# Fused attention and two expert layers: the opening pair taken head by head, maxima ordered by head, conversions spread over steps

## The chip, the cores and the metric

The kernel runs on one core of one Trainium2 chip. A core has TensorE (PE, the matrix engine, with PEld for its weight loads), VectorE (DVE), ScalarE (ACT), GpSimd (POOL) and SyncE (SP, which here only issues transfers). They run their own instruction queues in order and wait for each other by semaphores. The metric is the device time of one execution in microseconds; lower is better.

## The reference

```
q_pool = q.reshape(B, H, S // 2, 2, D).mean(axis=3)      # B 4, H 8, S 1152, D 64
scores = matmul(q_pool, k^T) / sqrt(D);  scores -= max(scores, axis=-1)
attn   = exp(scores);  attn /= sum(attn, axis=-1) + 1e-9
x      = matmul(attn, v), heads side by side               # 2304 tokens x 512
x      = (h - tanh(h)) @ w_out,      h = x @ w_in          # d_ff 2048
out    = (h * sigmoid(1.702 h)) @ w_out2, h = x @ w_in2
```

All products are carried in two parts: an operand is split into a rounded high part and the rest (names ending in h and l), and three products stand for one. The expert weights come as 64-bit numbers and are put together from their two 32-bit words by four bit operations on VectorE before they are split.

## The kernel before

**Pairs and steps.** The 32 heads are worked in 16 pairs, two heads side by side on the 128 partitions, head 0 of a pair on partitions 0 to 63 and head 1 on 64 to 127. A pair takes 18 steps, nine tiles of 128 keys for each head. In step g, `scores(g)` makes the transposed scores of one key tile for all 576 pooled queries (four products of 288 columns, lines 348 and 349) and ScalarE takes the exponential from the score banks twice, once whole (`pf`) and once rounded (`ph`). `rest(g-1)` subtracts the two (`pl`, line 372) on VectorE, or on GpSimd in steps 5 and 14. `pv(g-3)` multiplies with v: six products, or for each third tile two products in full precision that take the place of four (lines 394 and 384). The last one of a head is copied out by ScalarE (line 400, `u`).

**The row of maxima.** The negated maximum of each query is a 65th row of the second score operand (`q3`), so it has to be known before the scores. `max_tile(p, j, x)` multiplies one 128-column piece of the block-diagonal `bdqs` (both heads' queries) with half of the keys and VectorE reduces the result to one column of `mt` (lines 304, 308). 18 half tiles make a pair. Their PSUM pool holds one tile. `max_rows` takes the minimum of the two halves, transposes and sends the row by four transfers (line 324). For pairs from 2 on the half tiles stand one in a step, from step 13 of two pairs ahead to step 12 of the pair ahead; for pair 1 in the first 13 steps of pair 0; for pair 0 ahead of all, as nine whole tiles of three 384-column products.

**What sets the order.** Each engine's order is that in which the Python code calls; `plan` and `when` are tables of (pairs from the end or ahead, step) at which preparation of later pairs and the first eight expert weight blocks are called. `stack` sends a head's high and low parts into the score operands by six transfers on SyncE. The low part of k (`prep_kl`, line 284, on GpSimd) has one buffer, so it waits for the stack ahead of it. `normalise` (line 444) multiplies the finished pair by the reciprocals of its sums. Weight blocks are loaded by SyncE (line 123) into two buffers and converted by ScalarE (Abs, line 136), VectorE (lines 137, 141, 148, 152), ScalarE (line 159) and GpSimd (line 160), grouped as load, first two, last two, split.

Of the kernel before, what the change touches and what calls it, by code (L numbers as in the profile page):

```python
# [7 lines left out]
F32 = mybir.dt.float32  # L8
# [20 lines left out]
def tile_pooled_attention_two_moe(  # L29
# [72 lines left out]
    bdqs = [part(6 * S + i * S, QJ, 128) for i in range(2)]  # L102
# [26 lines left out]
    def convert_steps(raw, hi, lo, shape):  # L129
        box = {}  # L130

        def s0():
# [7 lines left out]
            )  # L140
            nc.vector.scalar_tensor_tensor(  # L141
                out=box["t"], in0=top, scalar=-0x40000000, in1=box["t"],
# [3 lines left out]
        def s1():  # L146
# [4 lines left out]
            )  # L151
            nc.vector.scalar_tensor_tensor(  # L152
# [13 lines left out]
        return [s0, s1, split] if raw.dtype == I32 else [s32]  # L166
# [6 lines left out]
    def piece(kind, n):  # L173
# [24 lines left out]
        return [ld, cv(0), cv(1), cv(2)]  # L198

    def attention(ctx: ExitStack):  # L200
# [18 lines left out]
        nc.vector.memset(f32(bdqs[0][:]), 0.0)  # L219
# [16 lines left out]
        def load_q(p):  # L236
            qraw[p] = ap.tile([128, 2, SP], F32, tag="qr", name="qr")
            nc.sync.dma_start(out=qraw[p], in_=q[p // NPB, p % NPB])

        def load_k(p):  # L240
            kraw[p] = ap.tile([128, S], F32, tag="kr", name="kr", bufs=2)
            nc.sync.dma_start(out=kraw[p], in_=k[p // NPB, p % NPB])
# [5 lines left out]
        def prep_qs(p, eng=None):  # L248
# [8 lines left out]
            (eng or nc.vector).tensor_add(pairs[p]["qs"], qraw[p][:, 0], qraw[p][:, 1])  # L257
# [8 lines left out]
        def prep_bdq(p, s):  # L266
            r = slice(64 * s, 64 * s + 64)
            nc.scalar.activation(
                bdqs[p % 2][r, :, r],
                pairs[p]["qs"][r, :].rearrange("p (j c) -> p j c", j=QJ), AF.Copy)  # L270
# [4 lines left out]

        def first_bdq():
            for s in range(2):
                r = slice(64 * s, 64 * s + 64)
                x = [qraw[0][r, e].rearrange("p (j c) -> p j c", j=QJ) for e in range(2)]
                nc.vector.tensor_add(bdqs[0][r, :, r], *x)  # L280
# [18 lines left out]
        def max_tile(p, j, x=0, pool=None, parts=2, n=HB):  # L299
            d = pairs[p]  # L300
            mx = (pool or ps_mx).tile([128, parts, 512], F32, tag="mx", name="mx")
            for a in range(parts):
                k0 = (x * parts + a) * n
                nc.tensor.matmul(  # L304
                    mx[:, a, 0:n], bdqs[p % 2][:, j, :], d["kh"][:, k0:k0 + n],
# [5 lines left out]
        def max_rows(p, queues=(nc.sync, nc.sync)):  # L311
            d = pairs[p]
            tt = ap.tile([128, 32], F32R, tag="tt", name="tt", bufs=2)
            if p > 0:
                mt = d["mt"]
                nc.vector.tensor_tensor(
                    mt[:, 0:QJ], f32(mt[:, 0:QJ]), f32(mt[:, 16:16 + QJ]), op=ALU.min)
# [484 lines left out]
```

## Time and profile before

| | us |
|---|---|
| time before, median of 3 runs (lowest, highest) | 1352.25 (1352.02, 1352.96) |
| the profiled execution: its time; its span | 1352.21; 1350.4 |
| PE busy in the span (share) | 1299.2 (96%) |
| DVE busy | 993.7 (74%) |
| ACT busy | 749.0 (55%) |
| POOL busy | 353.7 (26%) |

The span runs from the first to the last instruction of the profiled execution; its time is 1.8 us longer. Matmuls are pipelined and an instruction's end is modelled, so the distance from one start to the next says more on PE than a duration. In rows of a timeline the first number is the start, the second the time from the start of a group to its end, then engine, line, operation, output and inputs, count, and in brackets how long the engine had stood idle and what it waited for. PEclk is the granted clock as a share of full speed.

### The profile page before, as it was taken

How to read it: one execution, taken by the hardware profiler on the slowest of the kernel's cores; microseconds unless marked ns; L12 is line 12 of the kernel's file. 1: busy time of each engine (PE TensorE's matmuls, PEld its weight loads, DVE VectorE, ACT ScalarE, POOL GpSimd, SP SyncE). 2: the span in 40 equal slices, each digit the busy share in tenths (PEclk: the TensorE clock that was granted, in tenths of full speed). 3: DMA queues.
4: the chain of work that ended last, by engine and by line, in shares of the span. 5: the costliest groups of instructions: out<-in, count | busy, mean ns of one | idle time of the engine just before them, and what ended most of it. 6: DMA issues, size and time to landing. Idle time of an engine off the chain costs nothing.

```text
span 1350.4 us, 18699 instructions
## 1 busy us (share of the span) xinstructions
PE 1299.2 (96%) x6999; PEld 1154.7 (86%) x6999; DVE 993.7 (74%) x1242; ACT 749.0 (55%) x1143; POOL 353.7 (26%) x275
## 2 busy tenths in 40 slices
PE   5899999999999998989999999999999999999998
PEld 3899999999989987879889889888788888888887
DVE  6677777778887876899999999999843555645433
ACT  2577777777777766767665655666533322222211
POOL 6123333232333334224333333323110110110000
PEclk9999999999999998999999999999999999999999
DMA  7466666666666562111111111111111111111002
GB/s 186 121 166 169 163 165 170 167 164 155 162 150 173 128 144 63 57 48 32 47 48 32 48 47 32 47 48 32 48 47 32 47 47 32 60 35 32 24 32 86
DMA packets 59129, 117.56 MB, mean 87 GB/s; under 512 B 24992, under 2 KB 29088, under 8 KB 59040
## 3 DMA queue, kind: packets, MB, share of 16 engines
q1 hardware_dynamic: 59004, 116.38, 32.5%
q8 instruction: 55, 0.90, 0.3%
q14 instruction: 34, 0.28, 0.1%
q10 hardware_dynamic: 36, 0.00, 0.0%
HBM read 66.58 MB, written 4.79 MB: 53 GB/s over the span
## 4 chain that ended last, share of the span: by engine, by line
PE 55%; DVE 26%; ACT 7%; issue 4%; SPq 3%; DMA 3%; POOL 1%; DVEq 0%; ACTq 0%; POOLq 0%
PE y L697 16%; PE h L604 14%; PE pv L394 8%; PE mx L304 5%; PE pv L384 5%; PE sc L349 4%; PE sc L348 4%; DVE gg L661 3%; DVE mt L308 3%; DVE xb L710 2%; DVE wt L141 2%; DVE gg L645 2%; DVE wt L137 2%; DVE wt L148 2%; DVE wt L152 2%
## 5 line engine op out<-in xcount | busy, mean ns | idle before, releaser
L308 DVE TENSOR_REDUCE mt<-mx 128x1 fp32r<-128x576 f32 (+1 forms) x279 | 215.9, 775 | 99.7 <-PE mx L304 95.8
L354 ACT ACTIVATE pf<-sc 128x576 f32<-128x576 f32 x288 | 188.5, 654 | 150.0 <-PE sc L349 132.9
L604 PE MATMUL h<-hl,big 128*128 128x512 f32 (+1 forms) x940 | 211.6, 377 | 0.0
L604 PEld LDWEIGHTS h<-hl,big 128*128 128x128 f32 x940 | 174.0, 188 | 28.6
L348 PE MATMUL sc<-q,big 128*128 128x288 f32 x576 | 185.4, 335 | 1.5 <-DVE mt L308 1.5
L697 PE MATMUL y<-g,big 128*128 128x512 f32 (+1 forms) x780 | 177.4, 370 | 6.3 <-POOL g L616 5.4
L697 PE MATMUL y<-big,g 128*128 128x512 f32 x702 | 174.1, 392 | 3.2 <-DVE xb L710 3.2
L349 PE MATMUL sc<-q,a 65*128 65x288 f32 x576 | 165.6, 301 | 2.0 <-DMA q<-tt 2.0
L697 PEld LDWEIGHTS y<-g,big 128*128 128x128 f32 x780 | 141.8, 188 | 28.9 <-POOL g L616 8.1
L616 POOL TENSOR_TENSOR g<-gg,g 128x1024 fp32r<-128x1024 f32 (+1 forms) x40 | 87.7, 2191 | 275.5 <-ACT g L614 267.8
L697 PEld LDWEIGHTS y<-big,g 128*128 128x128 f32 x702 | 132.7, 189 | 31.1 <-DVE xb L710 3.6
L304 PE MATMUL mx<-kh,big 128*128 128x288 f32 (+1 forms) x567 | 134.5, 322 | 23.8 <-DVE mt L308 16.8
L372 DVE TENSOR_TENSOR pl<-pf,ph 128x576 fp32r<-128x576 f32 x160 | 146.2, 915 | 3.3 <-PE sc L349 1.8
L394 PE MATMUL pv<-ph,big 128*128 128x288 f32 x768 | 142.9, 297 | 5.6 <-ACT u L400 5.6
L614 ACT ACTIVATE g<-gg 128x1024 fp32r<-128x1024 f32 (+1 forms) x80 | 78.0, 974 | 115.8 <-PE y L697 105.7
L604 PE MATMUL h<-hl,w 128*128 128x512 f32 (+1 forms) x564 | 127.0, 377 | 0.0
L304 PEld LDWEIGHTS mx<-kh,big 128*128 128x128 f32 x567 | 95.0, 199 | 36.6 <-DVE mt L308 28.7
L160 POOL TENSOR_TENSOR big<-wt,big 128x512 fp32r<-128x512 f32 x46 | 67.7, 1480 | 219.8 <-ACT big L159 219.8
L710 DVE TENSOR_TENSOR xb<-xb,y 128x512 f32<-128x512 f32 (+1 forms) x114 | 71.1, 654 | 70.0 <-PE y L697 70.0
L394 PEld LDWEIGHTS pv<-ph,big 128*128 128x128 f32 x768 | 117.0, 190 | 6.0 <-ACT u L400 5.8
L364 ACT ACTIVATE ph<-sc 128x576 fp32r<-128x576 f32 x186 | 121.3, 652 | 0.0
L604 PEld LDWEIGHTS h<-hl,w 128*128 128x128 f32 x564 | 104.4, 188 | 17.1
(80 smaller groups left out, 2105.9 us busy)
## 6 DMA issues: line engine op xcount, KB each, us to landing
raw<-in_moe_w_in_dram SPq DMA_DIRECT2D x32, 512.0 KB
raw<-in_moe_w_out_dram SPq DMA_DIRECT2D x32, 512.0 KB
qr<-in_q_dram SPq DMA_DIRECT2D x16, 576.0 KB
kr<-in_k_dram SPq DMA_DIRECT2D x16, 576.0 KB
big<-kh SPq DMA_DIRECT2D x32, 288.0 KB
q<-qh SPq DMA_DIRECT2D x64, 144.0 KB
big<-kl SPq DMA_DIRECT2D x32, 288.0 KB
a<-kh SPq DMA_DIRECT2D x32, 288.0 KB
```

What stands on the lines that cost most here:

```text
L304: nc.tensor.matmul(mx[:, a, 0:n], bdqs[p % 2][:, j, :], d["kh"][:, k0:k0 + n], start=True, stop=True)
L308: nc.vector.tensor_reduce(d["mt"][:, c:c + 1], mx[:, :, 0:n], AX.XY, ALU.max, negate=True)
L348: nc.tensor.matmul(sc[:, x, 0:HB], a1[:, ks], q2[:, xs], start=True, stop=False)
L349: nc.tensor.matmul(sc[:, x, 0:HB], a2[:, ks], q3[:, xs], start=False, stop=True)
L354: nc.scalar.activation(both(pf), sc[:, :, 0:HB], AF.Exp, scale=SCALE)
L364: nc.scalar.activation(both(ph), sc[:, :, 0:HB], AF.Exp, scale=SCALE)
L372: eng.tensor_tensor(pl, pf, f32(ph[:]), op=ALU.subtract)
L394: nc.tensor.matmul(accs[hd][x], w[:, t, :], r[:, x * HB:(x + 1) * HB], start=(t == 0 and n == 0), stop=(t == KT - 1 and n == 2))
L604: nc.tensor.matmul(hb[:, j, 0:TBS[b]], wi[:, c, w, :], x[r][c], start=(k == 0), stop=(k == 3 * NKC - 1))
L616: eng.tensor_tensor(gt[:, :, 1, :], g, f32(gt[:, :, 0, :]), op=ALU.subtract)
L697: nc.tensor.matmul(ys[m][:, 0:w], lhsT, rhs, start=(fp == 0 and k == 0), stop=(fp == 1 and k == 5))
L710: nc.vector.tensor_add(dst, dst, ys[m][:, 0:w])
```

## The change

- `bdqs` is laid out by head: columns 0 to 575 are head 0's queries, 576 to 1151 head 1's, and a 128-column piece is cut across (piece 4 holds both heads). Head 0's row is then complete after five of nine pieces, and `max_rows(p, s)` is called for one head at a time: head 0 at step 13 of the pair ahead, head 1 at step 3 of the pair itself, four transfers each.
- The half tiles of a pair stand in 18 steps that begin at step 4 of the pair ahead, nine steps later than before.
- Pair 0 is opened by head: q and k are loaded in halves of 64 partitions, head 0's maxima are taken from `qh` and `kh` themselves (`first_max`, five tiles), then one tile of head 1; head 1's other eight half tiles stand in steps 0 to 2, with two PSUM buffers.
- `keep_warm(n)` issues n products of 512 columns on the zeroed `bdqs[1]` into a bank that nobody reads: 11 ahead of the first tile, one behind each tile of head 0, 14 behind head 1's first.
- Pair 0 and 1 have a table of their own (`opening`). In the others `stack(n, 1)` moves from step 13 to step 10, `normalise` is halved onto steps 2 and 5, some of the rest moves by a step.
- The four bit operations of a weight block are four calls and each has its own step; all loads and steps of the first eight blocks are placed anew. In the expert layers they are grouped as before (`joined`).
- GpSimd takes five subtractions in pair 0, two in the middle pairs, none in pair 15, and there four roundings instead of six.

```diff
-    bdqs = [part(6 * S + i * S, QJ, 128) for i in range(2)]
+    bdqs = [part(6 * S + i * S, S) for i in range(2)]
...
-        return [s0, s1, split] if raw.dtype == I32 else [s32]
+        return [shift, sign, flush, tail, split] if raw.dtype == I32 else [s32]
...
+        def first_max(s, j, x, pool, parts, n):
+            d = pairs[0]
+            r = slice(64 * s, 64 * s + 64)
+            m = min(128, SP - 128 * j)
+            mx = pool.tile([128, parts, 512], F32, tag="mx", name="mx")
+            for a in range(parts):
+                k0 = (x * parts + a) * n
+                nc.tensor.matmul(
+                    mx[0:m, a, 0:n], d["qh"][r, 128 * j:128 * j + m], d["kh"][r, k0:k0 + n],
+                    start=True, stop=True)
+            c = 16 * x + 5 * s + j
+            nc.vector.tensor_reduce(
+                d["mt"][0:m, c:c + 1], mx[0:m, :, 0:n], AX.XY, ALU.max, negate=True)
...
-        POOL_SUB = (5, 14)
-        pool_cast = range(NPAIR * NS - NS + 2, NPAIR * NS, 3)
+        pool_sub = {0: (5, 8, 11, 14, 17), NPAIR - 1: ()}
+        pool_cast = [(NPAIR - 1) * NS + i for i in (3, 6, 9, 12)]
...
-            ("o", 1, (-2, 14), (-1, 1), (-1, 3), (-1, 5)),
+            ("o", 1, (-2, 4), (-1, 5), (-1, 6), (-1, 7), (-1, 8), (-1, 9)),
...
+        q_sum(nc.vector, "qh", low)
+        k_high(nc.scalar, low, 0)
+        k_high(nc.gpsimd, low, 1)
+        q_sum(nc.vector, "qs", low)
+        nc.vector.tensor_sub(d0["ql"][low], d0["qs"][low], f32(d0["qh"][low]))
+        k_low(low, 0)
+        k_low(low, 1)
+        stack(0, 0)
...
+            def keep_warm(n):
+                for _ in range(n):
+                    nc.tensor.matmul(
+                        warm, bdqs[1][:, 0:128], bdqs[1][:, 0:512], start=True, stop=True)
+
+            keep_warm(11)
+            for j in range(5):
+                first_max(0, j, 0, ps_first, 3, 384)
+                keep_warm(1)
+            new_pair(1)
+            prep_kh(1, 0)
+            prep_kh(1, 1)
+            max_rows(0, 0, (nc.sync, nc.scalar, nc.sync, nc.scalar))
+            first_max(1, 0, 0, ps_first, 3, 384)
+            keep_warm(14)
+        load_v(0, 0)
+        prep_v(0, 0)
+        load_q(1)
+        stack(0, 1)
...
-                at = (n - 1) * NS - 5 + h if n > 1 else 13 * h // 18
-                max_at[at] = max_at.get(at, ()) + ((n, *divmod(h, 2)),)
+                max_at.setdefault(NS * n - 14 + h, []).append(
+                    lambda n=n, h=h: max_tile(n, *divmod(h, 2)))
...
+            (1, 2): [(stack, 0)], (1, 3): [(prep_v, 0)], (1, 10): [(stack, 1)],
+            (1, 12): [(prep_v, 1)], (1, 13): [(max_rows, 0)], (0, 3): [(max_rows, 1)],
...
-            if p > 1 and i == 4:
-                normalise(p - 2)
+            if p > 1 and i in (2, 5):
+                normalise(p - 2, [i // 3])
```

PE's queue from its first product to step 3 of pair 0, before (mx is a maximum tile, sc a score tile, pv the value banks):

```order
L304 MATMUL mx<-kh,big 128x384 x27
L348 MATMUL sc<-q_0_79,big 128x288
L349 MATMUL sc<-q_0_80,a_0_78 128x288
L348 MATMUL sc<-q_0_79,big 128x288
L349 MATMUL sc<-q_0_80,a_0_78 128x288
L304 MATMUL mx<-kh,big 128x288 x4
```

And now; warm is the bank of the zero products:

```order
L568 MATMUL warm<-big 128x512 x11
L338 MATMUL mx<-kh,qh 128x384 x3
L568 MATMUL warm<-big 128x512
...
L338 MATMUL mx<-kh,qh 64x384 x3
L568 MATMUL warm<-big 128x512
L338 MATMUL mx<-kh,qh 128x384 x3
L568 MATMUL warm<-big 128x512 x14
L392 MATMUL sc<-q_0_79,big 128x288
L393 MATMUL sc<-q_0_80,a_0_78 128x288
L392 MATMUL sc<-q_0_79,big 128x288
L393 MATMUL sc<-q_0_80,a_0_78 128x288
L338 MATMUL mx<-kh,qh 128x288 x6
```

Nine tiles ahead of the first score have become six with zero products between them, and three half tiles a step follow the first scores.

VectorE's queue in steps 2 to 7 of a middle pair with a weight block under conversion, before (xb is the normalised output, wt the weight under conversion):

```order
L308 TENSOR_REDUCE mt_90<-mx 128x1 x2
L372 TENSOR_TENSOR pl<-pf,ph 128x576
L308 TENSOR_REDUCE mt_90<-mx 128x1
L372 TENSOR_TENSOR pl<-pf,ph 128x576
L444 TENSOR_TENSOR xb_64<-u,rbd 128x320
L444 TENSOR_TENSOR xb_65<-u,rbd 128x256
L308 TENSOR_REDUCE mt_90<-mx 128x1 x2
L137 TENSOR_SCALAR wt<-raw 128x512
L141 SCALAR_TENSOR_TENSOR wt<-raw,wt 128x512
L308 TENSOR_REDUCE mt_90<-mx 128x1
```

And now, in steps 2 to 6:

```order
L328 TENSOR_REDUCE mt_90<-mx 128x1
L493 TENSOR_TENSOR xb_64<-u,rbd 128x320
L328 TENSOR_REDUCE mt_90<-mx 128x1
L416 TENSOR_TENSOR pl<-pf,ph 128x576
L351 TENSOR_TENSOR mt_90<-mt_90 128x5
L356 STREAM_TRANSPOSE tt<-mt_90 128x32
L328 TENSOR_REDUCE mt_92<-mx 128x1
L416 TENSOR_TENSOR pl<-pf,ph 128x576
L328 TENSOR_REDUCE mt_92<-mx 128x1
L493 TENSOR_TENSOR xb_65<-u,rbd 128x256
L328 TENSOR_REDUCE mt_92<-mx 128x1
L137 TENSOR_SCALAR wt<-raw 128x512
```

The two halves of the normalisation have moved apart, onto steps without a subtraction, the minimum and transpose of head 1 have come in at step 3, and one bit operation stands where there were two.

SyncE's queue from the row transfers (tt) of pair 15 on, before (raw is a weight block):

```order
L324 DMA q_0_80<-tt 1x9x32 x2
L324 DMA q_1_83<-tt 1x9x32 x2
L292 DMA big<-kh 64x1152
L293 DMA q_1_82<-qh 64x576
L294 DMA big<-kl 64x1152
L295 DMA q_1_82<-qh 64x576
L296 DMA a_1_81<-kh 64x1152
L297 DMA q_1_83<-ql 64x576
L123 DMA raw<-in_moe_w_out_dram 128x1024 x2
```

And now, from the first of these two weight loads (step 4 of pair 14) on, to head 1's row in step 3 of pair 15:

```order
L123 DMA raw<-in_moe_w_out_dram 128x1024
...
L312 DMA big<-kh 64x1152
L313 DMA q_1_82<-qh 64x576
L314 DMA big<-kl 64x1152
...
L478 DMA rbd<-rd 64x576 x2
L367 DMA q_0_80<-tt 1x5x32 x2
L367 DMA q_0_80<-tt 1x4x32 x2
L123 DMA raw<-in_moe_w_out_dram 128x1024
L367 DMA q_1_83<-tt 1x4x32 x2
L367 DMA q_1_83<-tt 1x5x32 x2
```

One of the two loads now stands ahead of the last stack and the last rows, the other between the two rows.

## Rows read from the trace of the kernel before

**Rows 1.** Windows: length, busy time of PE, PEld, DVE, ACT, POOL, PEclk, DMA.

```profile
58.00:504.00 446.00, 438.61 (x2941) 412.69 (x2940) 357.88 (x515) 320.71 (x567) 145.48 (x134) 1.00 0.63 157
...
537.00:1350.40 813.40, 796.38 (x3748) 687.02 (x3746) 579.84 (x659) 388.76 (x509) 170.40 (x97) 1.00 0.14 43
```

**Rows 2.** The page, 40 slices of the span: granted clock in tenths.

```profile
PEclk9999999999999998999999999999999999999999
```

**Rows 3.** The chain that ended last: start, length, what.

```profile
39.66 0.24 PE sc L349
...
45.38 0.14 PE sc L349
...
80.86 0.97 PE pv L384 x4
...
85.84 0.97 PE pv L384 x4
```

**Rows 4.** Timeline of PE in pair 0.

```profile
24.41 0.58 PE L349 MATMUL sc<-q,a 65*128 65x288 f32 x1 [1.99 <-DMA q<-tt]
...
57.77 0.29 PE L348 MATMUL sc<-q,big 128*128 128x288 f32 x1
```

**Rows 5.** Timelines of DVE and then SyncE, opening.

```profile
1.05 1.02 DVE L219 MEMSET big<- 128x1152 f32 x1 [1.05 <-PEq L787]
...
4.82 1.52 DVE L280 TENSOR_TENSOR big<-qr 64x576 fp32r<-64x576 f32 x2 [2.67 <-DMA qr<-in_q_dram]
...
17.62 2.62 DVE L308 TENSOR_REDUCE mt<-mx 128x1 fp32r<-128x1152 f32 x2 [0.16 <-PE mx L304]
...
21.79 0.21 DVE L318 STREAM_TRANSPOSE tt<-mt 128x32 f32<-128x32 f32 x1
...
33.95 0.76 DVE L257 TENSOR_TENSOR qs<-qr 128x576 f32<-128x576 f32 x1 [2.80 <-DMA qr<-in_q_dram]
...
28.73 1.25 SPq L238 DMA_DIRECT2D qr<-in_q_dram  x1
```

**Rows 6.** Timelines of PE, DVE and POOL in middle pairs.

```profile
109.31 0.53 PE L304 MATMUL mx<-kh,big 128*128 128x288 f32 x2 [0.20 <-DVE mt L308]
...
139.99 0.53 PE L304 MATMUL mx<-kh,big 128*128 128x288 f32 x2 [0.22 <-DVE mt L308]
...
341.35 0.52 PE L304 MATMUL mx<-kh,big 128*128 128x288 f32 x2 [1.04 <-DVE mt L308]
...
130.43 0.75 DVE L372 TENSOR_TENSOR pl<-pf,ph 128x576 fp32r<-128x576 f32 x1
...
135.67 1.52 DVE L372 TENSOR_TENSOR pl<-pf,ph 128x576 fp32r<-128x576 f32 x1
...
338.81 1.81 DVE L152 SCALAR_TENSOR_TENSOR wt<-raw,wt 128x512 int32<-128x512 int32 x1
...
131.68 3.32 POOL L284 TENSOR_TENSOR kl<-kr,kh 128x576 fp32r<-128x576 f32 x2 [6.05 <-DMA big<-kl]
```

**Rows 7.** Timelines of SyncE, ACT, DVE and PE around pair 15.

```profile
503.65 2.03 SPq L123 DMA_DIRECT2D raw<-in_moe_w_out_dram  x2
...
508.88 0.68 ACT L136 ACTIVATE wa<-raw 128x512 f32<-128x512 f32 x1 [6.20 <-DMA raw<-in_moe_w_out_dram]
...
509.35 0.69 DVE L141 SCALAR_TENSOR_TENSOR wt<-raw,wt 128x512 int32<-128x512 int32 x1
...
510.45 0.85 PE L394 MATMUL pv<-ph,big 128*128 128x288 f32 x2 [5.61 <-ACT u L400]
...
537.27 1.92 PE L604 MATMUL h<-big,w 128*128 128x384 f32 x10
```

**Rows 8.** Windows: one of two us in pair 15, columns as in Rows 1.

```profile
514.00:516.00 2.00, 2.00 (x8) 1.71 (x7) 1.86 (x4) 0.47 (x1) 0.00 (x0) 0.50 0.98 194
```

**Rows 9.** Timeline of SyncE in pair 2.

```profile
123.20 3.05 SPq L324 DMA_DIRECT2D q<-tt  x4
...
130.46 0.72 SPq L297 DMA_DIRECT2D q<-ql  x1
```

More of the change, by code (lines that the diff above doesn't have):

```diff
@@ L196, in cv, with joined, together @@
             return go
-        return [ld, cv(0), cv(1), cv(2)]
+        return [ld] + [cv(j) for j in range(5)]
+    def joined(jobs, parts=((0,), (1, 2), (3, 4), (5,))):
+        def together(js):
+            return lambda: [jobs[j]() for j in js]
+        return [together(js) for js in parts]
     def attention(ctx: ExitStack):
@@ L218, in whole, with refill @@
             return t % 3 == 1
-        nc.vector.memset(f32(bdqs[0][:]), 0.0)
+        nc.vector.memset(f32(bdqs[1][:]), 0.0)
+        def refill(i):
+            for old, new in zip((*vt[0], vfs[0]), (*vt[i], vfs[i])):
+                nc.scalar.activation(new[:, :, D:128], old[:, :, D:128], AF.Copy)
+            row = [stacks[x][1][D:D + 1, :] for x in (0, i)]
+            nc.scalar.activation(row[1], row[0], AF.Copy)
         def fill(i):
@@ L234, in attention, with load_q, load_k @@
         qraw, kraw, vraw, pairs = {}, {}, {}, {}
[L236 to L242, printed above, removed]
+        def load_q(p, rows=(slice(0, 128),)):
+            if p not in qraw:
+                qraw[p] = ap.tile([128, 2, SP], F32, tag="qr", name="qr")
+            for r in rows:
+                nc.sync.dma_start(out=qraw[p][r], in_=q[p // NPB, p % NPB][r])
+        def load_k(p, rows=(slice(0, 128),)):
+            if p not in kraw:
+                kraw[p] = ap.tile([128, S], F32, tag="kr", name="kr", bufs=2)
+            for r in rows:
+                nc.sync.dma_start(out=kraw[p][r], in_=k[p // NPB, p % NPB][r])
         def load_v(p, s):
@@ L471, in attention @@
                 lambda c=c: split_x(0, [c], nc.gpsimd if c < 2 else nc.vector))
-        load_q(0)
-        load_k(0)
-        fill(0)
-        fill(1)
-        first_bdq()
-        prep_qs(0)
-        prep_kh(0, 0)
-        nc.gpsimd.tensor_scalar(
-            out=pairs[0]["kh"][:, SP:S], in0=kraw[0][:, SP:S],
-            scalar1=1.0, scalar2=1.0, op0=ALU.mult, op1=ALU.mult)
-        prep_qh(0)
-        prep_ql(0)
+        low, high = slice(0, 64), slice(64, 128)
+        load_q(0, [low])
+        load_k(0, [low])
@@ new lines, in attention, with q_sum, k_high @@
+        load_q(0, [high])
+        load_k(0, [high])
+        load_k(1)
+        fill(0)
+        new_pair(0)
+        d0 = pairs[0]
+        def q_sum(eng, out, r):
+            eng.tensor_add(d0[out][r], qraw[0][r, 0], qraw[0][r, 1])
+        def k_high(eng, r, x):
+            c = slice(x * SP, (x + 1) * SP)
+            if eng is nc.scalar:
+                eng.activation(d0["kh"][r, c], kraw[0][r, c], AF.Copy)
+            else:
+                eng.tensor_scalar(
+                    out=d0["kh"][r, c], in0=kraw[0][r, c],
+                    scalar1=1.0, scalar2=1.0, op0=ALU.mult, op1=ALU.mult)
@@ L514, in attention @@
         load_k(2)
+        nc.gpsimd.memset(f32(bdqs[0][:]), 0.0)
+        fill(2)
         ps_sc = ctx.enter_context(tc.tile_pool(name="ps_sc", bufs=2, space=PSUM))
[L516 to L517 removed]
+        ps_two = ExitStack()
+        ps_mx = ps_two.enter_context(tc.tile_pool(name="ps_two", bufs=2, space=PSUM))
         total = NPAIR * NS
         max_at = {}
+        for h in range(8):
+            max_at.setdefault(h // 3, []).append(
+                lambda h=h: first_max(1, 1 + h // 2, h % 2, ps_mx, 2, HB))
```

167 lines of the change are left out of this document (86 added, 81 removed), and 14 rows, old and new, of the table when.

## Prediction, made before the changed kernel ran

> **What bounds the kernel now.** I read the time in three stretches of the attention part and one for the rest. The rest, the two expert layers from 537 us on, is 813.4 us long in [rows 1] and the change leaves its code as it is, so I count it as equal. TensorE (PE) is the engine that sets the end: in the middle stretch it is busy 438.6 of 446 us [rows 1]. So only time in which PE stands, or runs at its lower clock, can be won.
>
> The clock is read first, because the page hides it. Its row of granted clock begins with nines [rows 2], yet the chain of waits has one score product of 288 columns take 0.24 us at 39.7 and 0.14 us at 45.4 [rows 3]: 288 columns at 1.2 and at 2.4 GHz. So PE ran at its lower level until about 41.5 us, whatever the column says; that it can show the lower level is seen later, where a wait of 5.61 us is followed by 0.50 [rows 7, 8]. The Trainium skill, "TensorE: Matmul & The Clock Gate", section "Part 1: The HAM clock gate", says that the lower state is the default and activity ends it, and that profile records of it were seen unreliable; the spacing agrees. Were the column right, about 5 us of the first term below (ten of products between 24 and 41.5, at half speed) would not be there to win.
>
> At the higher level three steps (two with six value products, one with four) start 4.98 us after each other (85.84 less 80.86 in [rows 3]), 1.66 a step and 29.9 a pair. A score, maximum or value product of 288 columns is 0.135.
>
> **The first term: the opening, up to step 12 of pair 0, which starts at 57.77 [rows 4].** Before, nine reductions of 1.31 us each (2.62 for two) run until 21.8, the transpose ends at 22.0 and the scores go on at 24.41 [rows 4, 5]. After, head 0 alone is needed.
> - The zero products need only the memset, done at 2.07 [rows 5]. Eleven of 512 columns at 0.43 (by 0.24 for 288) last to 6.8. The half loads of q and k carry together what q alone did, whose sum started at 4.82 [rows 5]; with a conversion of 0.7 the operands are there at 5.5. So the zero products are what comes last, by 1.3, and PE starts its maxima at 6.8. They cost no more than that; 14 later ones lie in the wait for the row.
> - VectorE (DVE) does three half sums of 0.76 from 4.82 and is free by 7.1. First reduction at 8.2 (three products and their tail), five of 1.31, transpose 0.21: 15.0, against 22.0.
> - The row takes 2.4 (22.0 to 24.41): scores at 17.4. The 14 zero products stand behind head 1's first tile, whose buffer the fourth reduction frees at about 13.4; at 0.215 each they end near 17, so they are hidden. At the lower level they would end at 20.4.
> - Steps 0 to 2 hold eight reductions of 0.68. Between the first four and the rest DVE's order has the q sum of pair 1, whose load stands on SyncE's queue behind two row transfers and two of v: issued at about 17.5. The nearest row, a load in the same crowd, is 28.73 to 33.95, 5.2 us [rows 5]: 22.7, while DVE is ready at 20.2. A wait of 2.5 comes back here; queued behind it are four reductions and the bank release for the first value products. Four or five reductions, a subtraction of 0.75 and the sum itself: value products start at 27.6.
> - Eight steps of 1.66 and one value group of 0.8 follow: 41.7. The q load of pair 2 waits on SyncE behind a v load that waits for GpSimd, so I add 0.8: 42.5. Won: 57.8 - 42.5 = 15.3.
> Bounds: with both q loads in time, 19; with the clock lost, 9 (rival 1).
>
> **The second term: the middle, 446 us [rows 1].** 14.5 pairs of 29.9 make 433. Before has its maxima nine steps earlier and so eight half tiles fewer in this stretch (8 x 0.27 = 2.1): its floor is 431, and 15 us are stalls. Two kinds carry them. One comes once a pair: 139.99 less 109.31 is 30.68, 0.8 over the floor; there are 14. Ahead of it a DVE subtraction beside GpSimd takes 1.52 where it mostly takes 0.75, a second follows, then the normalisation, and the reduction is late for a maximum buffer that is single [rows 6]. The other sits at conversions: the fourth operation of one takes 1.81, where 0.69 is usual, and the maximum product waits 1.04 [rows 6].
>
> After, I walked one pair with these durations. The normalisation is in two halves, at steps 2 and 5, which have no subtraction on DVE and stand idle for some 0.8. The second stack of a pair is sent at step 10 instead of 13, so GpSimd's low part of k (3.32, [rows 6]) comes right behind its subtraction of step 14, clear of steps 0 to 3. The second minimum and transpose, 0.4 us at step 3, fit. A pair without conversions then has no stall: 0.8 won, nine times. In the five pairs with conversions the fourth operation stands at step 15 beside GpSimd's subtraction (1.81 again), and the subtraction of step 16 beside the low part of k: I get a stall of 0.3 and one of 0.6 in each, 4.5 in sum. With 0.7 for GpSimd's backlog in pair 1 the stretch is 433.3 + 5.2 = 438.5. Won: 7.5. If the stalls only move, it is 448, a loss of 2; if all go, 12.7 won.
>
> **The third term: pair 15 from step 3 to its end, 504.0 to 537.27, 33.3 us [rows 7].** 18 value groups and 15 score groups without maxima are 18 x 1.66 - 18 x 0.27 - 3 x 0.54 = 23.4. The other 9.9: SyncE issues two weight loads only at 503.65, behind the row transfers and the stack of pair 15; ScalarE meets its Abs of the first at step 1 and stands until 508.88, with the copy-out of the value banks behind it; PE stands 5.61 and then runs at the lower level until 516, which costs some 2.8 [rows 7, 8]. A late GpSimd subtraction is most of what is left. After, that load is issued at step 4 of pair 14, ten steps earlier, and first read at step 5 of pair 15. The stall has no other cause that stands ready behind it: the row of head 1 and the last loads are ahead. What comes in: one maximum product pair (0.27) and twelve DVE pieces of the last three conversions (7.5 us), one a step, hidden under steps of 1.4 where DVE has 0.67 of subtraction; GpSimd beside it slows some twofold. I allow 1.5. Won: 33.3 - 25.2 = 8.1; between 5 (DVE late all through) and 9.9.
>
> **The sum.** 15.3 + 7.5 + 8.1 = 30.9. Span 1350.4 - 30.9 = 1319.5; the profiled execution took 1352.21, 1.8 over its span, and the median of the runs is 1352.25: 1321.
>
> **Rivals.**
> 1. The clock does not hold in the opening. For: waits of 2.5 on DVE in steps 0 to 2 let PE stand two or three us, and 5.61 was enough for 0.50 [rows 7, 8]; five max tiles with one zero product each fill only half of PE. Against: after 41.5 us waits of 0.85 did nothing. The 14 products end 3.1 later and another dense stretch at the lower level, as from 510 to 516, costs about 3: first term 9, 1328. The Trainium skill states such a rule on the same page, section "HAM oscillation — how this bites in real kernels": bursts with waits between them start at the low clock each time; by it this rival holds.
> 2. The middle's stalls move but stay: the slowed conversion and the 0.4 at step 3 keep DVE late. Second term -2: 1331.
> 3. Everything fits: 19 + 12.7 + 9.9, 1311.
> 4. Slower. Head 1's row is now sent at step 3 and read at step 9, 9.4 us later. Four row transfers take SyncE 3.05 and 2.4 to land, behind six of a stack that take 4.9 [rows 9]. If the stack starts at the end of step 17 that leaves over 2 us; if it starts only in step 2, as before, nothing, and each us late costs 15 pairs an us. From 2.3 us a pair the kernel is slower: at 2.5, 1359.
>
> **Chances.** Forecast 0.52 (1315 to 1327 alone), rival 1 0.18, rival 2 0.13, both together (1337) 0.05, rival 3 0.05, rival 4 0.07. The range 1311 to 1333 leaves out both together, rival 4 and some tails. A change of 0.2% (2.7 us) is about what the runs can tell from none. Faster 0.93, which is all but rival 4; within it 0.03, where rival 4 just eats the gain; slower 0.04.
>
> **What would show it.** First score group at 17 to 18 us; score products 0.14 apart from about 9 us on, if not rival 1; DVE waiting for qr some 2 us at 20; step 12 of pair 0 near 42; pairs without conversions 29.9 apart, with them about 30.8; no wait for raw near pair 15; last value product 31 us earlier; expert layers 813. Wrong it would be by row waits at step 9, PE at 0.24 past 25 us, or DVE late at the start of the expert layers.

## The result, and the profile after

The changed kernel took 1333.32 us (median of four runs, 1330.18 to 1336.33; before 1352.18): a ratio of 0.9863, interval 0.9838 to 0.9888. It is faster, but by 19 us and not by 31, and lies just over the top of the range. The page of its profiled execution, span 1333.5: busy time, TensorE's row, granted clock and DMA in 40 slices.

```profile
PE 1299.0 (97%) x7036; PEld 1158.0 (87%) x7036; DVE 991.6 (74%) x1279; ACT 751.3 (56%) x1151; POOL 367.3 (28%) x273
...
PE   8899999999999999999999999999999999999998
...
PEclk8899999999999999999999999999999999999999
DMA  7776677777867731211110111111211111111012
```

TensorE's busy time did not change (1299.2 before), so what was won is standing time. I cut both traces at the same products: first score of step 12 of pair 0, first score of step 3 of pair 15, first expert product.

| stretch | before | after | won | forecast |
|---|---|---|---|---|
| opening, up to step 12 of pair 0 | 57.77 | 53.57 | 4.2 | 15.3 |
| middle, up to step 3 of pair 15 | 446.37 | 441.54 | 4.8 | 7.5 |
| end of pair 15 | 33.13 | 26.26 | 6.9 | 8.1 |
| expert layers | 813.1 | 812.1 | 1.0 | 0 |

The four gains add up to 16.9, the difference of the two spans.

The windows of the last three stretches after, columns as in [rows 1]:

```profile
53.57:495.11 441.54, 435.68 (x2960) 414.69 (x2959) 354.47 (x550) 318.86 (x568) 154.65 (x134) 1.00 0.70 161
495.11:521.37 26.26, 24.71 (x160) 22.48 (x159) 24.90 (x33) 19.92 (x39) 14.89 (x12) 1.00 0.13 38
521.37:1333.50 812.13, 795.68 (x3746) 687.19 (x3744) 580.38 (x660) 388.56 (x509) 171.58 (x98) 1.00 0.14 43
```

**The opening** is where most is missing. TensorE's timeline after (mx by line 338 is a maximum tile of pair 0, by line 324 of a later pair):

```profile
2.12 5.06 PE L568 MATMUL warm<-big 128*128 128x512 f32 x11 [2.12 <-DVE big L230]
...
13.96 5.04 PE L568 MATMUL warm<-big 128*128 128x512 f32 x14
18.84 0.29 PE L392 MATMUL sc<-q,big 128*128 128x288 f32 x1
...
26.20 0.85 PE L338 MATMUL mx<-kh,qh 64*128 64x288 f32 x2 [3.20 <-DVE mt L342]
...
30.57 0.82 PE L438 MATMUL pv<-ph,big 128*128 128x288 f32 x2
...
43.52 0.85 PE L324 MATMUL mx<-kh,big 128*128 128x288 f32 x2 [4.52 <-DVE mt L328]
```

Scores begin at 18.84 (forecast 17.4) and value products at 30.57 (27.6). TensorE's two long waits, 3.20 and 4.52, are VectorE standing at a sum of q, as its rows say. SyncE's rows, with one of GpSimd's behind them, show when the load of the second went out and what it stood behind:

```profile
24.72 0.76 DVE L280 TENSOR_TENSOR qs<-qr 128x576 f32<-128x576 f32 x1 [2.38 <-DMA qr<-in_q_dram]
...
41.39 1.41 DVE L280 TENSOR_TENSOR qs<-qr 128x576 f32<-128x576 f32 x1 [4.30 <-DMA qr<-in_q_dram]
```

```profile
26.70 6.21 SPq L267 DMA_DIRECT2D vr<-in_v_dram  x2
32.96 0.42 SPq L263 DMA_DIRECT2D kr<-in_k_dram  x1
33.48 0.38 SPq L257 DMA_DIRECT2D qr<-in_q_dram  x1
```

```profile
30.67 0.80 POOL L377 TENSOR_SCALAR big<-vr 128x384 fp32r<-128x384 f32 x1 [10.16 <-DMA vr<-in_v_dram]
```

The q of pair 2 is called behind two v loads. The second of these waits 6 us for its buffer. GpSimd converts that late because it stood 10.16 us for an earlier v load itself. Then k goes ahead of q, and q is used 7.9 us behind its issue. Behind each wait TensorE works at its lower level, 288 columns in 0.24 us. It was at that level ahead of the scores, too: the 14 zero products took 4.88 us from start to first score, where 3.0 were forecast. The granted clock of the first part of these, and of the stretches behind the two waits:

```profile
13.96:16.00 2.04, 2.04 (x6) 1.65 (x6) 1.90 (x3) 0.52 (x1) 1.62 (x2) 0.50 0.65 138
26.98:34.78 7.80, 7.80 (x30) 6.62 (x29) 6.50 (x10) 4.29 (x7) 4.03 (x4) 0.52 0.55 122
45.67:48.59 2.92, 2.92 (x14) 2.78 (x13) 0.91 (x2) 1.22 (x3) 0.00 (x0) 0.58 0.60 174
```

**The middle.** The stalls of [rows 6] are gone. Instead a score waits for a row of maxima in eight pairs, 5.7 us in sum, the longest in pair 7:

```profile
246.67 0.37 PE L393 MATMUL sc<-q,a 65*128 65x288 f32 x1 [1.48 <-DMA q<-tt]
```

### The profile page after: what moved, and what is told of

Read it like the earlier page. It is cut to its first block, busy times and chain, and to the rows that moved or that the text cites. A ratio compares the mean times of both kernels' runs of the same rounds, so it can differ in the third digit from the quotient of the medians.

```text
span 1333.5 us, 18898 instructions
## 1 busy us (share of the span) xinstructions
PE 1299.0 (97%) x7036; PEld 1158.0 (87%) x7036; DVE 991.6 (74%) x1279; ACT 751.3 (56%) x1151; POOL 367.3 (28%) x273
## 4 chain that ended last, share of the span: by engine, by line
PE 53%; DVE 23%; DMA 11%; ACT 7%; issue 5%; SPq 1%; POOL 1%; DVEq 0%; POOLq 0%; ACTq 0%
PE y L784 15%; PE h L691 14%; PE pv L438 7%; PE pv L428 5%; PE sc L393 4%; PE mx L324 4%; PE sc L392 4%; DVE gg L748 3%; DMA a<-kh 3%; DMA kr<-in_k_dram 2%; DVE xb L797 2%; DVE gg L732 2%; DVE wt L143 2%; DVE wt L137 2%; DMA q<-ql 2%
## 5 line engine op out<-in xcount | busy, mean ns | idle before, releaser
L328 DVE TENSOR_REDUCE mt<-mx 128x1 fp32r<-128x576 f32 x270 | 203.7, 755 | 91.3 <-PE mx L324 86.7
L416 DVE TENSOR_TENSOR pl<-pf,ph 128x576 fp32r<-128x576 f32 x159 | 132.2, 831 | 0.6 <-POOL ph L405 0.6
L324 PE MATMUL mx<-kh,big 128*128 128x288 f32 x540 | 117.8, 300 | 4.6 <-DVE mt L328 4.5
L393 PEld LDWEIGHTS sc<-q,a 65*128 65x128 f32 x576 | 110.2, 191 | 13.1 <-DMA q<-tt 4.3
```

Of the source, the lines that this page charges most:

```text
L324: nc.tensor.matmul(mx[:, a, 0:n], bdqs[p % 2][:, 128 * j:128 * j + 128], d["kh"][:, k0:k0 + n], start=True, stop=True)
L328: nc.vector.tensor_reduce(d["mt"][:, c:c + 1], mx[:, :, 0:n], AX.XY, ALU.max, negate=True)
L393: nc.tensor.matmul(sc[:, x, 0:HB], a2[:, ks], q3[:, xs], start=False, stop=True)
L416: eng.tensor_tensor(pl, pf, f32(ph[:]), op=ALU.subtract)
```

## The experiments

Each time is the median of four to six executions, beside executions of the kernel before (medians 1351.5 to 1353.1). The runs were taken in five groups. The changed kernel itself moved from group to group, on the same chip too (1340.00 and 1334.47 below), so three of the groups have a run of it without an edit. It is called the control there. The first group, of four runs, and the last, of two, have none.

### The opening: queue, clock, zero products

The loads of q sent ahead:

```diff
+            load_q(1)
             max_rows(0, 0, (nc.sync, nc.scalar, nc.sync, nc.scalar))
...
-        load_q(1)
         stack(0, 1)
...
-        load_v(1, 0)
-        load_v(1, 1)
-        load_k(2)
...
-            (1, 0): [(sum_q,)], (2, 0): [(load_q,)], (1, 1): [(prep_bdq, 0)],
+            (1, 0): [(sum_q,)], (2, 0): [(load_q,)], (1, 1): [(prep_bdq, 0), (load_v, 0)],
...
-            (2, 5): [(prep_qs,)], (2, 6): [(prep_qh,)], (2, 7): [(prep_bdq, 0)],
+            (1, 4): [(load_v, 1)], (2, 5): [(prep_qs,)], (2, 6): [(prep_qh,), (load_k,)], (2, 7): [(prep_bdq, 0)],
```

> The changed kernel with the load of pair 1's q sent ahead of head 0's row (it stood behind it and two v loads) and the load of pair 2's q ahead of pair 1's v and pair 2's k, which follow in steps 1 to 6. Theory (order of SyncE's queue): VectorE's two waits for q, 2.38 at 24.7 and 4.30 at 41.4, go, and with them TensorE's 3.20 and 4.52 and part of the lower clock behind them (26.2 to 34.8 and 43.5 to 48.3): step 12 of pair 0 starts near 43 instead of 53.6, the time is 1322 to 1325. Rival (the transfers themselves are the limit, their engines being 88 to 99% busy in these stretches): q lands no earlier, or what now stands behind it (v, k, the stack) is late instead; under 3 us won, 1331 to 1333.

Measured: 1331.69 (1327.58 to 1337.00). In its profile, that of its slowest run, both q waits are gone and head 0 of pair 0 is copied out at 46.80; in the four profiles of the changed kernel it is at 51.04 to 53.77. So 4 to 7 us are won there, as the theory of the queue has it. But its pairs 0 to 3 then come 32.41, 30.40 and 33.67 apart (29.84, 30.77 and 30.04 in the changed kernel), and 7.4 us of waits for rows stand in the middle. Most of the gain was given back, as the rival has it; how much of the time is left can't be told without a control.

The waits filled with products that nobody reads:

```diff
...
+                if (g, nth) in ((1, 2), (6, 0)):
+                    fill_wait(g, 20 if g == 1 else 30)
                 job()
```

> The changed kernel with 20 products that nobody reads in TensorE's wait of 3.20 us in step 1 and 30 in the wait of 4.52 us in step 6, into the score bank of the next step. The waits themselves stay. Theory (the lower clock behind a wait costs apart from the wait): score products stay 0.14 apart behind both. Behind the second that gives back 2.4 us (half of 43.5 to 48.3); behind the first at most 1.5, since VectorE is busy 7.3 of the 8.8 us there: 1329 to 1331. Rival (VectorE or ScalarE sets the pace behind both waits, so the clock costs nothing): 1333, although the products are 0.14 apart.

Measured: 1337.94 (1331.50 to 1342.01), with no control beside it, so the time decides nothing. In the trace the products behind both stay 0.14 apart. The second wait itself moves from run to run, so I count from the maximum product that ends it to the copy-out: 8.12 us here (41.54 to 49.66), 9.54 to 10.92 in the four profiles of the changed kernel. So the lower level behind the second wait costs 1.4 to 2.8 us, which holds the 2.4 of the theory.

> The changed kernel without the 30 zero products. Theory (they give the higher level from 7 us on and so are worth what the forecast's first term says): the maxima, the first scores and all up to step 3 run at the lower level, products 0.24 apart until past 35 us; step 12 of pair 0 3 to 6 us later, 1337 to 1339. Rival (the level is lost at 22 us anyway, and VectorE's reductions set the pace ahead of it): no change or up to 1.3 us won, as the maxima can start at 5.5: 1332 to 1333.

Measured: 1341.88 (1336.66 to 1344.54), but with 9.3 us of waits for rows in its profile and the copy-out at 52.11, no later than with the zero products. Undecided; taken up again below.

### The late rows: three cures that failed

```diff
-            (1, 2): [(stack, 0)], (1, 3): [(prep_v, 0)], (1, 10): [(stack, 1)],
+            (1, 4): [(stack, 0)], (1, 5): [(prep_v, 0)], (1, 10): [(stack, 1)],
```

> The changed kernel with the first stack of the next pair sent at step 4 instead of 2, so behind head 1's row of step 3 on SyncE's queue, and its v conversion at step 5 instead of 3. Theory (the row stands behind six stack transfers): the eight waits of a score for the row at step 9, 5.7 us in the profile, go; 1327 to 1329. Rival (something else, such as GpSimd's low part of k that waits for the stack, is late by the two steps, and the stall comes back there): 1332 to 1334.

Measured: 1421.90 (1416.69 to 1429.88), ratio 1.052 (1.0495 to 1.0546). Both were wrong. In step 4 the stack now stands ahead of the sums (s) of the pair that has ended. GpSimd's step on them is late, VectorE's reciprocal behind that stands with all reductions behind it, and TensorE waits 14 times, 52.7 us, beside the wait for q in the opening. SyncE's row, then VectorE's:

```profile
114.03 1.30 SPq L452 DMA_DIRECT2D s<-u  x1
```

```profile
118.02 0.21 DVE L463 RECIPROCAL r<-r 128x9 f32<-128x9 f32 x1 [4.73 <-POOL r L461]
```

With the stack behind the sums, at step 6, alone and together with the q loads:

> The changed kernel with the next pair's first stack at step 6 instead of 2 (and its v conversion at 7 instead of 3): behind head 1's row of step 3, as in the run with the stack at step 4, but also behind the two transfers of the sums of step 4, which that run had pushed back. Theory (the row of head 1 is late since it shares the queue and the transfer engines with six stack transfers): the waits at step 9 go, pairs come 29.8 to 30.2 us apart, 5 to 9 us won: 1324 to 1328 and runs closer together than the 6 us of the changed kernel. Rival (the second stack at step 10 or k's low part is now what is late): pairs as long or longer, 1333 or more.

> Both edits together, the q loads of the opening sent ahead and the first stack at step 6. Theory (the first won 7 us in the opening and lost them again in rows that were late in pairs 1 to 3; with the stack out of the rows' way they stay won): 1316 to 1321. Rival (the transfer engines are what is full up to 60 us, so the gain of the opening is given back in pair 1 whatever the order): as the stack edit alone, within 3 us of it.

Measured: 1440.99 (1435.81 to 1441.09) and 1432.11 (1425.20 to 1437.01). Pairs are mostly 37 to 40 us apart; 68.5 us of the first run are waits for rows. I had the wrong row: 246.67 is 11.5 us behind the copy-out of pair 6's head 0 (235.18, step 12), so the score that waits stands at step 0 of a pair, and what is late is **head 0's row**, called at step 13 behind the second stack. Whatever moves the first stack back pushes the second one, and that row, back too. Here the row's transfers are issued from 170.63 on, and the score stands until 175.81:

```profile
157.00:171.00 14.00, 13.06 (x89) 12.20 (x87) 10.68 (x17) 9.00 (x16) 3.63 (x4) 1.00 1.05 233
```

```profile
175.81 0.58 PE L393 MATMUL sc<-q,a 65*128 65x288 f32 x1 [5.75 <-DMA q<-tt]
```

The share of 1.05 says that the transfer engines are full for all the 14 us ahead of that row.

> The changed kernel once more, with no edit, beside the others on their chip: 1330 to 1336 if the range of its first four runs is its own.

Measured: 1340.00 (1334.95 to 1342.26), seven over the first set. Two of its row waits, 1.90 at 125.14 and 1.70 at 312.77, are followed by the lower level, and so is one of 2.33 at 309.81 in the last control; the waits of up to 1.48 in the first profile are not. The pairs with these three are 33.4 to 34.0 long, all others of the changed kernel's four profiles at most 31.6. The row of the first, and the clock behind it:

```profile
125.14 0.37 PE L393 MATMUL sc<-q,a 65*128 65x288 f32 x1 [1.90 <-DMA q<-tt]
```

```profile
127.00:129.00 2.00, 2.00 (x9) 1.86 (x9) 0.82 (x2) 0.72 (x2) 0.00 (x0) 0.50 1.03 219
```

Rows issued from GpSimd's queue, head 0's alone, then both with the q loads ahead:

```diff
-        def max_rows(p, s, queues=(nc.sync,) * 4):
+        def max_rows(p, s, queues=None):
+            queues = queues or (nc.sync if s else nc.gpsimd,) * 4
```

> The changed kernel with the four transfers of head 0's row (step 13 of the pair ahead) issued by GpSimd instead of SyncE, in all pairs but pair 0. A correction first: the score that waits for a row in the changed kernel stands at step 0 of a pair, not at step 9 (94.33 is ten us behind the copy-out at 83.61, which is step 12), so it is head 0's row that is late, and it stands behind the second stack, which the change moved from step 13 to step 10. Theory (SyncE's queue is late: the row is called at step 13 and issued at 16 to 17): the waits at step 0 go and with them the lower clock behind the longest; pairs 29.8 to 30.2 apart; 8 to 13 us under the control of this call, and the runs within 4 us of each other. Rival (the row's few bytes are late in the transfer engines, which the stack fills): waits as before, within 3 us of the control.

> Both rows of every pair but the first issued by GpSimd, and the q loads of the opening sent ahead. Theory (the opening's gain of 7 us was given back by late rows at step 0 of pairs 1 and 2): it adds to the run above, 5 to 7 us under that and 14 to 19 under the control. Rival (the transfer engines are full up to 60 us and the gain of the opening is given back in pair 1 by whatever lands last): within 2 us of the run above.

Measured: 1386.49 (1381.15 to 1388.34) and 1374.29 (1373.58 to 1374.68); the control of this group is below. GpSimd now stands for the transpose, issues for 2.14 us, and its subtraction and k's low part follow late and run beside a subtraction of VectorE, which takes 3.36 us:

```profile
125.18 2.14 POOL L368 DMA_DIRECT2D q<-tt  x4 [2.78 <-DVE tt L357]
127.33 1.43 POOL L417 TENSOR_TENSOR pl<-pf,ph 128x576 fp32r<-128x576 f32 x1
128.71 2.80 POOL L304 TENSOR_TENSOR kl<-kr,kh 128x576 fp32r<-128x576 f32 x2
```

```profile
128.78 3.36 DVE L417 TENSOR_TENSOR pl<-pf,ph 128x576 fp32r<-128x576 f32 x1
...
132.06 0.74 DVE L328 TENSOR_REDUCE mt<-mx 128x1 fp32r<-128x576 f32 x1
```

The maximum product behind it waits 1.52. In the whole run TensorE stands 25.4 us at maxima and 12.6 at transfers of the stack. Neither theory had this. The Trainium skill, "SBUF — State Buffer", section "SBUF: two separate sides", says that where VectorE and GpSimd both need the pair of ports that they share, one of them holds it for its whole instruction and the other is blocked. The row agrees that VectorE was held, and shows more: its 0.75 became 3.36 and ended 0.63 behind the second of GpSimd's pieces, so it was held through two instructions.

> The changed kernel with no edit, beside the others on their chip. By the two sets so far 1330 to 1342. Its waits for a row should stand at step 0 of a pair, and where one is longer than about 1.7 us the products behind it should be 0.24 apart for some 3 us.

Measured: 1335.52 (1332.03 to 1338.05). All eight row waits stand at step 0 of a pair; the longest here is 1.47.

### The late rows: the cause

The second stack back behind the row, as it was before the change:

```diff
-            (1, 2): [(stack, 0)], (1, 3): [(prep_v, 0)], (1, 10): [(stack, 1)],
-            (1, 12): [(prep_v, 1)], (1, 13): [(max_rows, 0)], (0, 3): [(max_rows, 1)],
+            (1, 2): [(stack, 0)], (1, 3): [(prep_v, 0)], (1, 12): [(prep_v, 1)], (1, 13): [(max_rows, 0), (stack, 1)], (0, 3): [(max_rows, 1)],
```

> The changed kernel with the second stack of the middle pairs sent again at step 13 behind head 0's row, as in the kernel before. Theory (the stack's move to step 10 is what makes the row late): no wait for a row at step 0. But k's low part waits for that stack again, so GpSimd's 3.3 us slide into steps 0 to 3 and VectorE's subtraction there slows: waits of a maximum product for VectorE, some 0.3 to 0.8 a pair; the sum within 5 us of the control either way. Rival (the row is late for SyncE's load in all, not for its place): row waits stay, and the time is 5 or more over the control.

Measured: 1341.84 (1340.87 to 1344.04), 6.3 over its control, so a little more than the theory allowed. No row wait is left past the opening. Instead k's low part stands for the stack and the maxima wait in each pair, as in [rows 6]; GpSimd's row, then TensorE's:

```profile
94.25 3.33 POOL L304 TENSOR_TENSOR kl<-kr,kh 128x576 fp32r<-128x576 f32 x2 [5.44 <-DMA big<-kl]
```

```profile
101.09 0.53 PE L324 MATMUL mx<-kh,big 128*128 128x288 f32 x2 [0.34 <-DVE mt L328]
```

So the stack's move takes one stall away and makes the other. Why there is no room for both is seen in pair 6 of the changed kernel: SyncE, and then windows of steps 4 to 7, 8 to 12, 13 to 15 and 16 to 17, where the share of the transfer engines is the last number but one:

```profile
218.34 0.64 SPq L317 DMA_DIRECT2D q<-ql  x1
223.05 2.78 SPq L367 DMA_DIRECT2D q<-tt  x4
...
228.82 0.57 SPq L257 DMA_DIRECT2D qr<-in_q_dram  x1
229.49 0.38 SPq L267 DMA_DIRECT2D vr<-in_v_dram  x1
229.92 0.42 SPq L263 DMA_DIRECT2D kr<-in_k_dram  x1
...
242.17 3.36 SPq L367 DMA_DIRECT2D q<-tt  x4
```

```profile
221.60:228.30 6.70, 6.70 (x47) 6.33 (x45) 5.23 (x11) 5.28 (x10) 1.93 (x2) 1.00 0.11 24
228.30:236.60 8.30, 8.30 (x61) 8.04 (x60) 5.95 (x10) 7.14 (x14) 1.51 (x3) 1.00 0.77 213
236.60:241.60 5.00, 5.00 (x36) 4.79 (x36) 4.64 (x9) 3.16 (x6) 1.48 (x2) 1.00 1.05 208
241.60:245.20 3.60, 3.59 (x24) 3.15 (x22) 2.71 (x5) 2.09 (x4) 3.50 (x3) 1.00 0.83 161
```

SyncE stands from 218.98 to 223.05 at head 1's row, until VectorE has transposed it, with the sums of the pair that has ended and the loads of q, v and k behind it; the transfer engines run nearly empty (0.11). Then loads and second stack come at once (1.05), and head 0's row goes out from 242.17 on, three us behind its transpose (239.09 to 239.30). So k's load was put ahead of head 1's row:

```diff
             (2, 16): [(prep_kl, 0)], (2, 17): [(prep_kl, 1)], (3, 5): [(load_q,)],
-            (3, 9): [(load_k,)], (3, 17): [(prep_qs,)],
+            (3, 2): [(load_k,)], (3, 17): [(prep_qs,)],
```

> The changed kernel with the load of k for three pairs ahead at step 2 instead of 9, so ahead of head 1's row on SyncE's queue. In the changed kernel the transfer engines stand at a mean share of 0.02 to 0.34 in steps 4 to 7 of pairs 4 to 11 and at 0.9 to 1.05 in steps 9 to 15, where head 0's row is to go out. Theory (SyncE stands at head 1's row until VectorE has transposed it, with the loads behind it, and these 590 KB then bunch up ahead of the second stack and the row): the share at steps 4 and 5 rises, that at 13 to 15 falls, the row at step 13 is issued earlier, the waits at step 0 fall from 6.5 to 10 us in sum to under 2; 5 to 8 us under the control, runs within 4 us. Rival (head 1's row, or the stack of step 10, is now late behind k, or GpSimd holds SyncE at the buffer of k): the waits move to step 9, time as the control or more.

> The changed kernel with no edit, beside the others on their chip: 1330 to 1342.

Measured: 1328.60 (1326.63 to 1329.17); the control 1334.47 (1331.47 to 1339.93). 5.9 us won, and no score waits for a row any more. Pairs without conversions come 29.82 to 29.84 apart. The row goes out right behind its transpose (236.07 to 236.28), and the share ahead of it is below full:

```profile
236.46 2.79 SPq L367 DMA_DIRECT2D q<-tt  x4
```

```profile
235.00:240.00 5.00, 5.00 (x35) 4.77 (x35) 3.92 (x8) 3.04 (x5) 2.69 (x2) 1.00 0.85 166
```

With the q loads of the opening ahead too, and `(3, 11): [(load_k,)]` of the opening at step 14:

> That edit together with the q loads of the opening sent ahead, and the k of pair 3 loaded behind pair 1's row (step 14 of pair 0 instead of 11). Theory (the 7 us that the q loads won up to step 12 of pair 0 were given back since the transfers that they pushed back bunched up ahead of the rows of pairs 1 to 3): 5 to 7 us under the run above, 1320 to 1326. Rival (the bytes of the opening fill the transfer engines up to 60 us, so the end of pair 1 stays where it is): within 2 us of the run above.

Measured: 1323.24 (1321.08 to 1325.09), ratio 0.9787 (0.9774 to 0.98): 5.4 under the run above, 11 under the control. The opening's gain stays once the rows are in time: the best version.

### The zero products, and the table

Two edits on that best version, whose runs lie close enough to tell:

```diff
-                for _ in range(n):
+                for _ in range(0):
```

> The best kernel so far (both q loads sent ahead, k at step 2; 1323.24, its runs 4 us apart) without the zero products. The first run without them was hidden in late rows. Theory (they hold the higher level through the opening, which the forecast put at 6.3 us, 15.3 less 9): 1328 to 1331, step 12 of pair 0 near 51 instead of 45.4. Rival (VectorE's reductions and the row's landing set the pace of the opening whatever the clock): step 12 within 1.5 us of 45.4, 1322 to 1325.

Measured: 1323.31 (1322.72 to 1323.71), ratio 0.979 (0.9776 to 0.9805): no difference that the runs can tell, though one of a us or two is not excluded. The copy-out in its profile is 2.2 us later (47.79, 45.55), less than half of what the theory asked for and more than the rival allowed. The first scores follow each other by 0.24, though the window's clock says 1.00:

```profile
23.38 0.44 PE L393 MATMUL sc<-q,a 65*128 65x288 f32 x1
23.62 0.44 PE L392 MATMUL sc<-q,big 128*128 128x288 f32 x1
```

```profile
20.00:24.00 4.00, 3.63 (x13) 2.68 (x11) 2.34 (x4) 1.19 (x2) 0.91 (x1) 1.00 0.96 206
```

With zero products the level is down from 14 to 17 (0.50), up at 20 and lost again from 24 to 31, so what they buy is gone when the dense work begins; I take that for the reason, but did not try it by itself.

The old table of conversions with its four groups, on the changed kernel, then on the best version:

```diff
-            ("i", 0, (-8, 0), (-8, 6), (-8, 8), (-8, 11), (-8, 15), (-8, 17)),
+            ("i", 0, (-8, 6), (-7, 6), (-7, 14), (-6, 7)),
...
-            for (o, i), job in zip(steps, piece(kind, f), strict=True):
+            for (o, i), job in zip(steps, joined(piece(kind, f)), strict=True):
```

> The changed kernel with the table of the last conversions of the kernel before and its four groups (load, two operations, two operations, split), all else as changed. Theory (the respread table is what took the wait for weight loads out of pair 15): the stretch from step 3 of pair 15 to the first expert product is 33 us again instead of 26.3, the time 1338 to 1342. Rival (it was that the last stack and row no longer stand ahead of these loads): the stretch stays at 26 to 28 and the time within 2 us of the changed kernel's.

> The best kernel so far with the old table of the last conversions and their four groups. In the changed kernel that cost 22 us beside the control, with 11.5 us of waits for rows among it. Theory (two operations called together hold VectorE past a step, and with the new order of the rest these meet the maxima each time): waits of a maximum product for VectorE of 1 to 3 us in the pairs with conversions, 12 to 18 us over the best kernel. Rival (the loss came from rows behind the weight loads, and those have room now): under 6 us over.

Measured: 1361.96 (1357.51 to 1367.69), 22 over its control and slower than before; and 1339.04 (1336.64 to 1340.99), 15.8 over the best version (15.7 over the run without zero products, taken beside it). In the second, three pairs grow to 34.3 to 34.6, each with one wait of 2.97 and the lower level behind it (0.50 from 329.89 to 332.00 in the first of them): two operations of one block follow each other on VectorE beside GpSimd, 3.7 us in sum. VectorE, then TensorE:

```profile
323.42 1.92 DVE L150 SCALAR_TENSOR_TENSOR wt<-wa,wt 128x512 f32<-128x512 f32 x1
325.38 1.77 DVE L157 SCALAR_TENSOR_TENSOR wt<-raw,wt 128x512 int32<-128x512 int32 x1
```

```profile
327.87 0.53 PE L324 MATMUL mx<-kh,big 128*128 128x288 f32 x2 [2.97 <-DVE mt L328]
```

Yet the end of pair 15 stays short in both, 26.1 in the first and 26.3 in the second (497.95 to 524.20). ScalarE stands 2.23 us for a weight block there in the second, but TensorE waits no more than 0.7 at any product.

The table alone, on the kernel before:

> The kernel before with one part of the change alone: the four bit operations as four calls and the new table of the first eight weight blocks (the expert layers grouped as before). The opposite run, the changed kernel with the old table, lost some 22 us in the pairs with conversions, and yet kept its stretch behind step 3 of pair 15 short, with no wait for a weight block there. Theory (the table is worth what it saves in the conversion pairs, where two operations called together hold VectorE; and here it also takes the two loads from behind the last rows): the long pairs come down from 32.0 to 32.4 to about 30.7, and the stretch from step 3 of pair 15 to the first expert product from 33.1 to 26 to 28; 1339 to 1343. Rival (the wait for the loads in the kernel before came from the last stack's place behind the rows, which stays): the stretch stays over 31 and the time over 1345.

Measured: 1348.98 (1344.62 to 1349.17), ratio 0.9966 (0.9952 to 0.9979), between the two. The end of pair 15 is 504.33 to 533.69, 29.4, without a wait for a load; the last late subtraction of GpSimd, 2.34, is still there. The conversion pairs were 31.3 to 32.4, hardly better: on the old order of the rest the maxima still meet them (waits of 0.7 to 1.5).

## Why the prediction was wrong, and where it was right

In all four sets of runs the changed kernel's median (1333.32, 1340.00, 1335.52, 1334.47) lies over the range, so the miss is not one of a single set.

**The step that failed** first is in the first term: "The q load of pair 2 waits on SyncE behind a v load that waits for GpSimd, so I add 0.8". It cost 4.52 of standing time and a stretch at the lower level behind it (43.5 to 48.3). I had seen the queue, but not added up what stood on it: the v load 6.2 us at its buffer, k ahead of q, and 7.9 us to land in full transfer engines (share 0.96 from 33.48 to 41.39). With the loads ahead (the best version) step 12 begins at 45.35: 12.4 won of the 15.3.

The other parts of that term. The wait for the q of pair 1 has the forecast size (2.38 for 2.5) by luck: the load took 7.5 us and not the 5.2 that I took from [rows 5], and VectorE was ready at 22.3 and not at 20.2, so both ends were two us late. The scores were 1.4 late, and that "they are hidden" was wrong for the 14 zero products: in the changed kernel's profile they end last, and no score waits for the row. In 13 of the 16 profiles that have them they took 4.4 to 5.9 us; in three, at the higher level, 3.3. In one of these three (the first stack at step 6) scores begin at 17.35 with the row there by 17.48, as forecast; in the other two the row comes at 18.70 and 18.92, and in the two runs without zero products the same score starts at 19.52 and 19.62 (the profile puts the first of these down to a load of v). So the row can take 4.0 to 4.6 from its transpose instead of 2.4, and either of the two can cost the 1.4; what made the row late was not tried. Rival 1 holds in part: the clock was lost in the opening, ahead of the scores in most runs and behind both waits for q. Without the zero products the time of the best version is the same.

**The second term** came out at 4.8 instead of 7.5, by a step that I counted as a gain alone: "The second stack of a pair is sent at step 10 instead of 13". It does what was said for GpSimd, and the stalls of [rows 6] went. But the stack now stands ahead of head 0's row, in a queue whose loads are bunched by head 1's row: 5.7 us of waits, of the 7.4 by which the best version's middle is shorter; in other runs the clock adds to that. Rival 4 had this mechanism, and its row, stack and step wrong: I priced head 1's. With that cured, pairs stand 29.82 apart (forecast 29.9) and the middle of the best version is 434.10: 12.3 won, the case in which all stalls go (12.7). Conversion pairs cost 0.4, not 0.9.

**The third term** had nearly the right size (6.9 for 8.1) and half the cause. Not the load's new place alone took the wait away: with the old table and the rest of the change it is gone too, and the stretch as short (26.1 and 26.3). The table alone takes the wait away as well, but leaves 29.4. Which part of the rest does it was not tried.

**The sum** of the best version by the same stretches: 12.4, 12.3, 6.9, and 0.4 lost in the expert layers, is 31.2, to the forecast's 30.9. That the sums agree so closely is partly luck, as the parts are off by 2.9, 4.8, 1.2 and 0.4 and cancel. But the floor of a pair was counted rightly, and 11 us of what the changed kernel lost beside that came back when loads were moved to the right side of a wait in SyncE's queue.

**The spread.** The changed kernel's runs lay 6 to 8.5 us apart and its medians 1333 to 1340. Those of the five versions in which the rows of the middle are in time (second stack back, k ahead, the best, and the best without zero products or with the old table) lie 1.0 to 4.4 apart. That a late row costs more or less by chance, now and then with the clock, fits this, and the profiles show it: the row waits add up to 5.7, 10.1, 6.5 and 8.0 us in the changed kernel's four, and three waits of 1.70 and more have the lower level behind them. What makes a row later in one run than in the next was not tried. With that spread, the 2.7 us that the prediction took for the least change that can be told were too few.

## What to carry to other kernels

When a row of a few hundred bytes is late, look at what its queue did before: a transfer that waits for its data holds every load behind it, the transfer engines run empty, and later all of it comes at once. Send loads whose buffer is free ahead of transfers that wait for an engine. And cost a moved step by each queue that it passes: the same move can mend one stall and make another of the same size.

## What the hardware showed beyond that

- One subtraction of VectorE, 0.75 alone, took 3.36 beside two pieces of GpSimd (2.80 together) and ended behind both.
- The higher level can be had early with products on zeros (scores 0.14 apart at 19 us, where they are 0.24 apart at 23 us without them), but it does not stay. In the best version two waits of 0.59 and 0.73 us in a stretch with little other work (20 to 24 us: TensorE busy 2.68 of 4) were followed by the lower one, 0.53 from 24.27 to 31.50. A wait of 1.48 in a full stretch of the changed kernel was not; waits of 1.70, 1.90 and 2.33 were.
